# Block-causal attention and a gated feed-forward in fp32: the last part of the feed-forward in chunks of 512 tokens instead of 256

## The chip, the cores and the metric

The kernel runs on one core of one Trainium2 chip. The metric is the time of one execution in microseconds (us) of device time; lower is better. The core has five engines, each with a queue of its own that is worked through strictly in program order: PE (TensorE: matrix products; PEld is its loading of weights), DVE (VectorE), ACT (ScalarE), POOL (GpSimd) and SP (SyncE, which here issues nearly all transfers). Matrix products are written to PSUM, a memory of eight banks; one bank holds 512 fp32 numbers on each of 128 partitions. Everything else on the chip lies in SBUF, and the DRAM beside the chip holds inputs, outputs and scratch.

## The reference, cut to what matters

```python
# attention: q, k, v are [8, 8, 576, 64] (batch, heads, sequence, head size)
scores = scale * np.matmul(q, k.transpose(0, 1, 3, 2))
mask = pos[:, None] // 64 >= pos[None, :] // 64
scores = np.where(mask, scores, -1000000000.0)
attn = np.exp(scores - np.max(scores, axis=-1, keepdims=True))
attn = attn / (np.sum(attn, axis=-1, keepdims=True) + 1e-09)
x = np.matmul(attn, v)          # transposed and reshaped to [4608, 512]
# feed-forward: w_in is [512, 2048], w_out is [2048, 512]
h = x @ w_in
P = a[0] + a[1] * h + a[2] * h * h + a[3] * h * h * h
Q = 1.0 + np.abs(b[0]) * np.abs(h) + np.abs(b[1]) * h * h
out = (P / (Q + 1e-6)) @ w_out  # [4608, 512]
```

## The kernel before

Products are made in three parts of reduced fp32 each (high by high, high by low, low by high), so each operand is kept as a high and a low half, and every product below comes as three matmuls.

**Attention** goes over 32 pairs of heads. Its result x is written to scratch in DRAM (`xscr`, one tile for each batch, high and low halves side by side, transposed so that the 512 features lie on partitions in four blocks `dc`).

**The feed-forward** (class `Ffn`) is cut twice. Over the 2048 hidden features in two phases: phase 0 takes the first 10 blocks of 128 (`NFA`), phase 1 the last 6 (`NFB`). Over the 4608 tokens in 18 chunks of 256 (`CT`, `NCH`). A unit is one chunk and two blocks, so a chunk has 5 units in phase 0 and 3 in phase 1 (`NU`): 90 and 54 units. Phase 0 runs between the steps of the attention as its batches are finished, and its last units run when the attention has ended; phase 1 runs after the attention as a whole. Each unit has four steps, and `steps` writes them down with a lag of one, two and three units:

- `first`: 24 matmuls (L200), 2 blocks x 4 feature blocks x 3 parts, each 128x128 weights against 256 tokens, into one PSUM bank `h`; then ACT (L207, L208), POOL (L209, L210) and DVE (L211, L212) work out numerator and denominator. L212 is the last reader of `h`.
- `recip`: ACT (L217, L222) and DVE (L223 to L225) divide; in phase 1 the reciprocal `r` lies in a PSUM bank as well.
- `split`: ACT (L232) and POOL (L233) make the high and low half `gh` and `gl`.
- `second`: 12 matmuls (L249) of 512 columns add the unit's share to `o`, one bank for each 128 tokens, so two in a chunk, `o0` and `o1`. After a chunk's last unit phase 0 copies `o` to `os` (L256) and writes it to scratch `pscr`; phase 1 reads that partial sum back into `pt` (one buffer), adds it on DVE (L262) and writes the output.

Tokens are read from `xscr` by `load` (L184): a chunk has two tiles `x` of two feature blocks each, out of one ring of three buffers (`XB`) in the pool `ffn`.

**PSUM**: five banks in `ps_a` (scores, transposes and `pv` of the attention; later every second `h`, and all `r`), one in `ps_h` (the other `h`), two in `ps_o`.

**What sets the order.** The kernel is written in a Python order, and a scheduler then decides, from a timeline of its own, in which order each engine's instructions stand; buffers and waits follow from that, and on the chip nothing passes anything else on the same engine. All transfers named here stand in SP's queue. The completion marks of its transfers go round in eight lanes, and a transfer may be issued when the one eight places ahead of it has landed. When the attention ends, its SBUF pools are given back and the pools `wB` (weights of phase 1, twelve transfers of 512 KB, L586) and `ffb` (second set of buffers for the feed-forward) are laid in the same place; nothing can be written there before the attention's last readers are through.

Names below are `h0_15_4`: tile h, phase 0, chunk 15, unit 4; `x0_15_1` is the second tile of tokens of chunk 15; `o31_1` is the last product of the attention (`pv` of pair 31).

Of the kernel before, what the change touches and what calls it, by code (L numbers as in the profile page):

```python
# [9 lines left out]
F32 = mybir.dt.float32  # L10
F32R = mybir.dt.float32r
# [33 lines left out]
CBUFS = 2  # L45
NFA = 10
NFB = NF - NFA
NU = (NFA // 2, NFB // 2)
LP = 96
NL = S // LP  # L50
QSCALE = 0.125
# [7 lines left out]
def attn_ffn_kernel(  # L59
# [14 lines left out]
    cpool = ctx.enter_context(tc.tile_pool(name="const", bufs=1))  # L74
    dpool = ctx.enter_context(tc.tile_pool(name="scratch", bufs=1, space=DRAM))
    ffn = ctx.enter_context(tc.tile_pool(name="ffn", bufs=2))
    ps_a = ctx.enter_context(tc.tile_pool(name="ps_a", bufs=5, space=PSUM))
    ps_h = ctx.enter_context(tc.tile_pool(name="ps_h", bufs=1, space=PSUM))
    ps_o = ctx.enter_context(tc.tile_pool(name="ps_o", bufs=1, space=PSUM))

# [85 lines left out]
    class Ffn:  # L166
# [6 lines left out]
            self.ready = 0  # L173

        def load(self, ph, c):
            self.x[ph, c] = []
            for i in range(2):
                x = ffn.tile([128, 2, 2, CT], F32R, name=f"x{ph}_{c}_{i}", tag="x", bufs=XB)
                t0 = c * CT
                while t0 < (c + 1) * CT:  # L180
                    b = t0 // S
                    t1 = min((c + 1) * CT, (b + 1) * S)
                    for d in range(2):
                        nc.sync.dma_start(out=x[:, d, :, t0 - c * CT:t1 - c * CT].bitcast(F32),  # L184
                                          in_=xscr[b][:, 2 * i + d, :, t0 - b * S:t1 - b * S])
                    t0 = t1
                self.x[ph, c].append(x)

        def first(self, ph, c, u):
            wih, wil, _, _ = self.w[ph]  # L190
            xs = self.x[ph, c]
            tag = f"{ph}_{c}_{u}"
            pool = self.pools[self.n % len(self.pools)]
            h = self.hpools[self.n % len(self.hpools)].tile([128, 2, CT], F32, name=f"h{tag}", tag="a")
            for j in range(2):
                f = 2 * u + j
                fs = slice(f * 128, (f + 1) * 128)
                for dc in range(4):
                    for i, (w, hl) in enumerate(((wih, 1), (wih, 0), (wil, 0))):
                        nc.tensor.matmul(h[:, j, :], lhsT=w[:, dc, fs], rhs=xs[dc // 2][:, dc % 2, hl, :],  # L200
                                         start=(dc == 0 and i == 0), stop=(dc == 3 and i == 2))
# [10 lines left out]
            nc.vector.scalar_tensor_tensor(out=st, in0=st, scalar=a1, in1=hf, op0=ALU.subtract, op1=ALU.mult)  # L212
            self.m[ph, c, u] = (pool, ut, vt, st)

        def recip(self, ph, c, u):
            pool, ut, vt, st = self.m[ph, c, u]
            nc.scalar.activation(out=vt, in_=ut, func=AF.Ln, bias=qcb)  # L217
            if ph == 1:
                r0 = ps_a.tile([128, 512], F32, name=f"r{ph}_{c}_{u}", tag="a")
            else:  # L220
                r0 = vt
            nc.scalar.activation(out=r0, in_=vt, func=AF.Exp, scale=-1.0)  # L222
            nc.vector.scalar_tensor_tensor(out=ut, in0=ut, scalar=QC, in1=r0, op0=ALU.add, op1=ALU.mult)  # L223
            nc.vector.scalar_tensor_tensor(out=r0, in0=ut, scalar=-2.0, in1=r0, op0=ALU.add, op1=ALU.mult)  # L224
            nc.vector.scalar_tensor_tensor(out=st, in0=st, scalar=a0, in1=r0, op0=ALU.subtract, op1=ALU.mult)  # L225

        def split(self, ph, c, u):
            pool, ut, vt, st = self.m.pop((ph, c, u))
            tag = f"{ph}_{c}_{u}"
            gh = pool.tile([128, 2, CT], F32R, name=f"gh{tag}", tag="gh", bufs=GBUFS if pool is ffn else 2)  # L230
            gl = pool.tile([128, 2, CT], F32R, name=f"gl{tag}", tag="gl", bufs=GBUFS if pool is ffn else 2)
            nc.scalar.copy(out=gh.rearrange("p j t -> p (j t)"), in_=st)  # L232
            nc.gpsimd.tensor_tensor(out=gl.rearrange("p j t -> p (j t)"), in0=st,  # L233
                                    in1=gh.rearrange("p j t -> p (j t)").bitcast(F32), op=ALU.subtract)
            self.g[ph, c, u] = (gh, gl)

        def second(self, ph, c, u):
            _, _, woh, wol = self.w[ph]
            gh, gl = self.g.pop((ph, c, u))
            nu = NU[ph]  # L240
            if u == 0:
                self.o = [ps_o.tile([128, DM], F32, name=f"o{ph}_{c}_{m}", tag=f"o{m}")
                          for m in range(2)]
            for j in range(2):
                f = 2 * u + j
                for m in range(2):
                    ms = slice(m * 128, (m + 1) * 128)
                    for i, (g, w) in enumerate(((gl, woh), (gh, woh), (gh, wol))):
                        nc.tensor.matmul(self.o[m], lhsT=g[:, j, ms], rhs=w[:, f, :],  # L249
                                         start=(u == 0 and j == 0 and i == 0),  # L250
                                         stop=(u == nu - 1 and j == 1 and i == 2))
            if u == nu - 1:
                osb = ffn.tile([128, 2, DM], F32, name=f"os{ph}_{c}", tag="os")
                if ph == 0:
                    for m in range(2):
                        nc.scalar.copy(out=osb[:, m, :], in_=self.o[m])  # L256
                    nc.sync.dma_start(out=pscr[c], in_=osb)
                else:
                    part = ffb.tile([128, 2, DM], F32, name=f"pt{c}", tag="pt", bufs=1)
                    nc.sync.dma_start(out=part, in_=pscr[c])  # L260
                    for m in range(2):
                        nc.vector.tensor_tensor(out=osb[:, m, :], in0=self.o[m], in1=part[:, m, :], op=ALU.add)  # L262
                    nc.sync.dma_start(out=out[c * CT:(c + 1) * CT, :].rearrange("(m p) d -> p m d", p=128),
                                      in_=osb)
                self.o = None

        def steps(self):
            units = [(ph, c, u) for ph in range(2) for c in range(NCH) for u in range(NU[ph])]
            l1, l2, l3 = LAG
            for i in range(len(units) + l3):  # L270
                if i < len(units):
                    if units[i][:2] not in self.x:
                        self.load(*units[i][:2])
                    if i + 1 < len(units):
                        ph, c, u = units[i + 1]
                        if u == 0 and c < self.ready:
                            self.load(ph, c)
                if 0 <= i - l2 < len(units):
                    self.split(*units[i - l2])
                if i < len(units):  # L280
# [338 lines left out]
```

## Time and profile before

| | |
|---|---|
| median of 3 runs | 1389.79 us (1387.79 to 1392.57) |
| the profiled execution, its own time | 1388.67 us |
| its span, first to last instruction | 1386.9 us |
| mean granted TensorE clock | 0.971 |
| matmuls of L200 (`first`) | 3456, of 128x256 |
| matmuls of L249 (`second`) | 1728, of 128x512 |
| attention's last matmul | starts at 980.63 us of the span |

How to read it: a profile is one execution. The views used below are the page's busy time of each engine; tables of the busy time in stretches of the span; the chain of waits, which starts at the last instruction and goes back, at each step, to what released it; the waits in total; and the timeline, instruction by instruction. A matmul's own duration holds the time in which it flows through the array beside its neighbours; what it costs in a stream is the distance from its start to the next one's.

### The profile page before, as it was taken

Reading aid. Unit: us, or ns where it says so; the run is one execution under the profiler, and the core shown is the slowest. Engines: PE = TensorE matmul, PEld = TensorE weight load, DVE = VectorE, ACT = ScalarE, POOL = GpSimd, SP = SyncE. Lnnn points to the kernel's source line nnn. Section 1 sums busy time; section 2 is a strip of 40 time slices with the busy share of each in tenths; the row PEclk is TensorE's granted clock in tenths of the full one; section 3 lists DMA queues with packets and bytes.
Section 4 is the critical chain, followed back from the end, with each engine's and each line's share of the span. In section 5 each row is a group of like instructions: output and inputs, shape, how many; then the busy total and the mean of one; then the engine's idle time right before and its main releaser. Section 6 shows DMA issues by size and latency. Waiting matters only on the chain.

```text
span 1386.9 us, 25820 instructions
## 1 busy us (share of the span) xinstructions
PE 1296.0 (93%) x8736; PEld 1190.8 (86%) x8736; DVE 1031.0 (74%) x2048; ACT 909.3 (66%) x2250; POOL 958.3 (69%) x1240
## 2 busy tenths in 40 slices
PE   4778799999899989999999999999989999999998
PEld 3667788999888889888989999999979999999897
DVE  5898877787678868877767777766756677777665
ACT  5766766777577766776777777776545655555553
POOL 4888987687677757777767676766556655556564
PEclk9687999999999999999999999999999999999999
DMA  9778555666556665675654565651711333333332
GB/s 221 191 195 236 147 150 160 168 168 181 147 136 154 163 167 140 156 171 140 168 134 110 153 149 126 150 141 44 263 55 61 107 122 122 122 122 122 122 122 91
DMA packets 225635, 200.93 MB, mean 145 GB/s; under 512 B 132064, under 2 KB 195552, under 8 KB 225504
## 3 DMA queue, kind: packets, MB, share of 16 engines
q1 hardware_dynamic: 225440, 199.28, 53.8%
q8 instruction: 70, 1.15, 0.3%
q14 instruction: 61, 0.50, 0.1%
q0 software_dynamic: 64, 0.00, 0.0%
HBM read 98.57 MB, written 44.04 MB: 103 GB/s over the span
## 4 chain that ended last, share of the span: by engine, by line
PE 70%; DVE 9%; POOL 8%; ACT 5%; DMA 4%; issue 2%; SPq 1%; POOLq 0%; ACTq 0%; DVEq 0%
PE h L200 25%; PE o L249 25%; PE o L488 9%; PE t L469 4%; PE s L420 3%; PE s L421 3%; PE tp L354 2%; ACT p L437 1%; DVE v L224 1%; POOL u L210 1%; DVE nm L425 1%; POOL p L450 1%; DMA x<-xscr 1%; POOL gl L233 1%; DVE u L223 1%
## 5 line engine op out<-in xcount | busy, mean ns | idle before, releaser
L200 PE MATMUL h<-x,wih 128*128 128x256 f32 x2304 | 442.6, 288 | 10.1 <-DMA x<-xscr 5.9
L200 PEld LDWEIGHTS h<-x,wih 128*128 128x128 f32 x2304 | 368.8, 192 | 19.6 <-issue 6.8
L200 PE MATMUL h<-x,wil 128*128 128x256 f32 x1152 | 329.5, 286 | 0.0
L249 PE MATMUL o<-woh,gl 128*128 128x512 f32 x576 | 233.0, 405 | 8.1 <-POOL gl L233 6.8
L209 POOL TENSOR_SCALAR v<-u,bab 128x512 f32<-128x512 f32 x144 | 119.7, 831 | 162.9 <-ACT u L207 160.8
L249 PE MATMUL o<-woh,gh 128*128 128x512 f32 x576 | 228.5, 397 | 0.0
L249 PE MATMUL o<-wol,gh 128*128 128x512 f32 x576 | 227.2, 395 | 0.0
L233 POOL TENSOR_TENSOR gl<-s,gh 128x512 fp32r<-128x512 f32 x144 | 188.4, 1309 | 51.4 <-ACT gh L232 48.3
L425 DVE TENSOR_REDUCE nm<-s 128x1 f32<-128x288 f32 (+4 forms) x384 | 161.7, 427 | 81.2 <-PE s L424 46.1
L200 PEld LDWEIGHTS h<-x,wil 128*128 128x128 f32 x1152 | 221.3, 192 | 0.5
L437 ACT ACTIVATE p<-s,nm 128x288 f32<-128x288 f32 (+4 forms) x384 | 184.6, 485 | 48.4 <-DVE nm L425 34.9
L210 POOL TENSOR_TENSOR u<-v,u 128x512 f32<-128x512 f32 x144 | 189.7, 1318 | 9.8
L450 POOL TENSOR_SCALAR p<-p,rc 128x128 f32<-128x128 f32 (+3 forms) x256 | 166.2, 660 | 30.0 <-DVE rc L445 28.3
L217 ACT ACTIVATE v<-u,qcb 128x512 f32<-128x512 f32 x144 | 104.6, 726 | 95.9 <-POOL u L210 95.1
L207 ACT ACTIVATE u<-h 128x512 f32<-128x512 f32 x144 | 86.0, 597 | 120.8 <-PE h L200 114.4
L420 PE MATMUL s<-kq 128*128 128x256 f32 (+3 forms) x384 | 138.3, 362 | 22.0 <-DMA kq<-hl 9.6
L211 DVE TENSOR_TENSOR s<-s,h 128x512 f32<-128x512 f32 x144 | 98.6, 684 | 68.7 <-ACT s L208 67.9
L249 PEld LDWEIGHTS o<-woh,gl 128*128 128x128 f32 x576 | 109.5, 190 | 28.9 <-POOL gl L233 9.3
L249 PEld LDWEIGHTS o<-wol,gh 128*128 128x128 f32 x576 | 109.1, 189 | 22.8
L249 PEld LDWEIGHTS o<-woh,gh 128*128 128x128 f32 x576 | 109.5, 190 | 16.0
L421 PE MATMUL s<-kq 128*128 128x256 f32 (+3 forms) x384 | 121.0, 317 | 0.0
L469 PE MATMUL t<-ident,p 128*128 128x128 f32 (+1 forms) x672 | 114.0, 280 | 6.2 <-DVE x L492 1.8
(105 smaller groups left out, 3031.9 us busy)
## 6 DMA issues: line engine op xcount, KB each, us to landing
kq<-hl SPq DMA_DIRECT2D x64, 432.0 KB, 4.2
x<-xscr SPq DMA_DIRECT2D x96, 256.0 KB, 3.6
kq<-hl SPq DMA_DIRECT2D x64, 288.0 KB, 5.3
xscr<-x SPq DMA_DIRECT2D x32, 320.0 KB, 4.2
qr<-in_q_dram SPq DMA_DIRECT2D x64, 144.0 KB, 2.8
kr<-in_k_dram SPq DMA_DIRECT2D x64, 144.0 KB, 2.9
kq<-hl SPq DMA_DIRECT2D x64, 144.0 KB, 4.8
pscr<-os SPq DMA_DIRECT2D x18, 512.0 KB, 3.2
```

Of the source, the lines that this page charges most:

```text
L200: nc.tensor.matmul(h[:, j, :], lhsT=w[:, dc, fs], rhs=xs[dc // 2][:, dc % 2, hl, :], start=(dc == 0 and i == 0), stop=(dc == 3 and i == 2))
L209: nc.gpsimd.tensor_scalar(out=vt, in0=ut, scalar1=b1, scalar2=b0, op0=ALU.mult, op1=ALU.add)
L210: nc.gpsimd.tensor_tensor(out=ut, in0=vt, in1=ut, op=ALU.mult)
L233: nc.gpsimd.tensor_tensor(out=gl.rearrange("p j t -> p (j t)"), in0=st, in1=gh.rearrange("p j t -> p (j t)").bitcast(F32), op=ALU.subtract)
L249: nc.tensor.matmul(self.o[m], lhsT=g[:, j, ms], rhs=w[:, f, :], start=(u == 0 and j == 0 and i == 0), stop=(u == nu - 1 and j == 1 and i = ...
L420: nc.tensor.matmul(ps[:, :ww], lhsT=kq[:, 0, qs], rhs=kq[:, 1, c0:c0 + ww], start=True, stop=False)
L421: nc.tensor.matmul(ps[:, :ww], lhsT=kq[:, 0, qs], rhs=kq[:, 2, c0:c0 + ww], start=False, stop=not last)
L425: nc.vector.reduce_max(out=nm[:nq, j, i:i + 1], in_=ps[:nq, :w], axis=AX.X, negate=True)
L437: nc.scalar.activation(out=pt[:nq, j, c0:c0 + w], in_=banks[i][:nq, :w], func=AF.Exp, bias=nm[:nq, j, 0:1], scale=1.0, accum_out=sm[:nq, j ...
L450: nc.gpsimd.tensor_scalar(out=pt[:nq, jj, 64:n], in0=pt[:nq, jj, 64:n], scalar1=rc[:nq, jj:jj + 1], scalar2=1.0, op0=ALU.mult, op1=ALU.mult)
L469: nc.tensor.transpose(ps[:, i, :nq], src, ident[:nq, :nq])
L488: nc.tensor.matmul(o[:, s0:w], lhsT=vblock(vv, x), rhs=pp, start=(x == 0 and i == 0), stop=(x == nb - 1 and i == 2))
```

## The change

Phase 1 takes 9 chunks of 512 tokens and units of one block of hidden features, 6 to a chunk; the number of units stays 54. `first` makes 12 matmuls of 512 columns instead of 24 of 256. `second` still makes 12, now for one block and four groups of 128 tokens, into four banks `o0` to `o3`. The scalar work of a unit has the same 128x512 shape as before. A chunk's end now makes two outputs of 256 tokens each, one after the other, through the one buffer `pt`.

PSUM: `ps_a` is given back with the attention; a new pool `ps_b` takes its five banks: three for every second `h` and for all `r`, one each for `o2` and `o3`.

Tokens: a tile of phase 1 is one feature block of 512 tokens, four to a chunk. Tiles are taken by turns from `ffn` and from the last of the pools in use, with three buffers in each. Once the attention has ended that last pool is `ffb`, for phase 0 too: the second tile of each chunk that is loaded from then on lies in `ffb`.

```diff
+CTS, NBU = (CT, 512), (2, 1)
+NU = (NFA // NBU[0], NFB // NBU[1])
+NCS = (NT // CTS[0], NT // CTS[1])
...
-    ps_a = ctx.enter_context(tc.tile_pool(name="ps_a", bufs=5, space=PSUM))
...
         def load(self, ph, c):
+            n = CTS[ph]
+            nd = 512 // n
...
-                x = ffn.tile([128, 2, 2, CT], F32R, name=f"x{ph}_{c}_{i}", tag="x", bufs=XB)
+            for i in range(4 // nd):
+                pool = (ffn, self.pools[-1])[i % 2]
+                x = pool.tile([128, nd, 2, n], F32R, name=f"x{ph}_{c}_{i}", tag="x", bufs=XB)
...
         def first(self, ph, c, u):
-            h = self.hpools[self.n % len(self.hpools)].tile([128, 2, CT], F32, name=f"h{tag}", tag="a")
-            for j in range(2):
-                f = 2 * u + j
+            hp = self.hpools[self.n % len(self.hpools)]
+            h = hp.tile([128, NBU[ph], CTS[ph]], F32, name=f"h{tag}", tag="a", bufs=1 if hp is ps_h else 3)
+            for j in range(NBU[ph]):
+                f = NBU[ph] * u + j
...
-                r0 = ps_a.tile([128, 512], F32, name=f"r{ph}_{c}_{u}", tag="a")
+                r0 = ps_b.tile([128, 512], F32, name=f"r{ph}_{c}_{u}", tag="a", bufs=3)
...
         def second(self, ph, c, u):
+            nm = CTS[ph] // 128
             if u == 0:
-                self.o = [ps_o.tile([128, DM], F32, name=f"o{ph}_{c}_{m}", tag=f"o{m}")
-                          for m in range(2)]
+                self.o = [(ps_o if m < 2 else ps_b).tile([128, DM], F32, name=f"o{ph}_{c}_{m}", tag=f"o{m}", bufs=1)
+                          for m in range(nm)]
...
             if u == nu - 1:
+                for k in range(nm // 2):
+                    c2 = c * nm // 2 + k
...
-                    part = ffb.tile([128, 2, DM], F32, name=f"pt{c}", tag="pt", bufs=1)
-                    nc.sync.dma_start(out=part, in_=pscr[c])
+                        part = ffb.tile([128, 2, DM], F32, name=f"pt{c2}", tag="pt", bufs=1)
+                        nc.sync.dma_start(out=part, in_=pscr[c2])
...
-                        if u == 0 and c < self.ready:
+                        if u == 0 and c < self.ready and ph < len(self.pools):
...
     with ExitStack() as actx:
+        ps_a = actx.enter_context(tc.tile_pool(name="ps_a", bufs=5, space=PSUM))
...
-    ff.pools, ff.hpools = [ffn, ffb], [ps_h, ps_a]
+    ps_b = ctx.enter_context(tc.tile_pool(name="ps_b", bufs=1, space=PSUM))
+    ff.pools, ff.hpools = [ffn, ffb], [ps_h, ps_b]
```

What the scheduler makes of it. Up to the end of the attention every engine's order is the same as before. **SP, at the end of the attention.** These rows are SP's transfers, destination first, from the last but one product of the attention to the first transfers behind the weights of phase 1 (`wih10` to `wol10`, four for each pair of blocks). Before:

```order
L493 DMA xscr7_80<-x30_1_13239 128x2x256
L184 DMA x0_15_1_13752<-xscr6_79 128x2x192 x2
L184 DMA x0_15_1_13752<-xscr7_80 128x2x64
L184 DMA x0_16_0_14038<-xscr7_80 128x2x256 x2
L493 DMA xscr7_80<-x31_0_13430 128x2x320
L184 DMA x0_15_1_13752<-xscr7_80 128x2x64
L493 DMA xscr7_80<-x31_1_13548 128x2x256
L586 DMA wih10_13712<-wih10_198 128x4x256
...
L586 DMA wol10_13715<-wol10_201 128x1024
L260 DMA pt0_15031<-pscr0_81 128x1024
L257 DMA pscr14_95<-os0_14_13977 128x1024
L184 DMA x0_16_1_14041<-xscr7_80 128x2x256 x2
```

With the change:

```order
L504 DMA xscr7_77<-x30_1_13239 128x2x256
L189 DMA x0_16_0_14042<-xscr7_77 128x2x256 x2
L189 DMA x0_17_0_14329<-xscr7_77 128x2x256 x2
L504 DMA xscr7_77<-x31_0_13430 128x2x320
L504 DMA xscr7_77<-x31_1_13548 128x2x256
L598 DMA wih10_13713<-wih10_198 128x4x256
...
L598 DMA wol10_13716<-wol10_201 128x1024
L189 DMA x0_15_1_13756<-xscr6_76 128x2x192 x2
L189 DMA x0_15_1_13756<-xscr7_77 128x2x64 x2
L267 DMA pscr14_92<-os0_14_13981 128x1024
L189 DMA x0_16_1_14045<-xscr7_77 128x2x256 x2
```

The second tile of chunk 15 moved from ahead of the twelve weight transfers to right behind them, since it now lies in `ffb`.

**PE, at the same place.** The rows are matmuls, from the last one of the attention; each group of rows with the same `h` or `o` is cut to its first. Before:

```order
L488 MATMUL o31_1_13520<-pt2h_132,vpl_135 128x256
L200 MATMUL h0_15_0_13816<-x0_15_0_13747,wih0_142 128x256
...
L200 MATMUL h0_15_0_13816<-x0_15_1_13752,wih0_142 128x256 x2
...
L200 MATMUL h0_15_1_13871<-x0_15_1_13752,wih0_142 128x256 x2
...
L200 MATMUL h0_15_2_13926<-x0_15_0_13747,wih0_142 128x256 x2
...
L249 MATMUL o0_14_0_13733<-woh0_144,gl0_14_4_13868 128x512
...
L200 MATMUL h0_15_4_14048<-x0_15_0_13747,wih0_142 128x256 x2
...
L200 MATMUL h0_15_3_13985<-x0_15_0_13747,wih0_142 128x256 x2
```

With the change:

```order
L499 MATMUL o31_1_13520<-pt2h_132,vpl_135 128x256
L256 MATMUL o0_14_0_13737<-woh0_144,gl0_14_4_13872 128x512
...
L206 MATMUL h0_15_0_13820<-x0_15_0_13751,wih0_142 128x256 x2
...
L206 MATMUL h0_15_2_13930<-x0_15_0_13751,wih0_142 128x256 x2
...
L206 MATMUL h0_15_4_14052<-x0_15_0_13751,wih0_142 128x256 x2
...
L206 MATMUL h0_15_0_13820<-x0_15_1_13756,wih0_142 128x256 x2
L206 MATMUL h0_15_0_13820<-x0_15_1_13756,wil0_143 128x256
L206 MATMUL h0_15_1_13875<-x0_15_1_13756,wih0_142 128x256 x2
```

Between the attention's last matmul and the first that reads `x0_15_1` there now stand 12 matmuls of `second` (unit `14_4`) and six of `first` for each of the units 0, 2 and 4 of chunk 15; before, whole units stood there, one after the other.

**SP, at the very end.** The rows are the last transfers of the program. Before:

```order
L184 DMA x1_17_1_17721<-xscr7_80 128x2x256 x2
L263 DMA out_0_dram<-os1_15_17780 128x2x512
L260 DMA pt16_17957<-pscr16_97 128x1024
L263 DMA out_0_dram<-os1_16_17956 128x2x512
L260 DMA pt17_18015<-pscr17_98 128x1024
L263 DMA out_0_dram<-os1_17_18014 128x2x512
```

With the change:

```order
L189 DMA x1_8_3_16956<-xscr7_77 128x2x512
...
L273 DMA out_0_dram<-os1_15_17140 128x2x512
L270 DMA pt16_17333<-pscr16_94 128x1024
L273 DMA out_0_dram<-os1_16_17332 128x2x512
L270 DMA pt17_17339<-pscr17_95 128x1024
L273 DMA out_0_dram<-os1_17_17338 128x2x512
```

The sequence of names is the same, but `os1_16` and `os1_17` now belong to one chunk: both are added up behind the chunk's last unit, so `pt17` is read back after the end of the matmuls and no longer during them.

More of the change, by code (lines that the diff above doesn't have):

```diff
@@ L47 @@
 NFB = NF - NFA
-NU = (NFA // 2, NFB // 2)
+CTS, NBU = (CT, 512), (2, 1)
+NU = (NFA // NBU[0], NFB // NBU[1])
+NCS = (NT // CTS[0], NT // CTS[1])
 LP = 96
@@ L175, in load @@
         def load(self, ph, c):
+            n = CTS[ph]
+            nd = 512 // n
             self.x[ph, c] = []
-            for i in range(2):
-                x = ffn.tile([128, 2, 2, CT], F32R, name=f"x{ph}_{c}_{i}", tag="x", bufs=XB)
-                t0 = c * CT
-                while t0 < (c + 1) * CT:
+            for i in range(4 // nd):
+                pool = (ffn, self.pools[-1])[i % 2]
+                x = pool.tile([128, nd, 2, n], F32R, name=f"x{ph}_{c}_{i}", tag="x", bufs=XB)
+                t0 = c * n
+                while t0 < (c + 1) * n:
                     b = t0 // S
[L182 to L185, printed above, removed]
+                    t1 = min((c + 1) * n, (b + 1) * S)
+                    for d in range(nd):
+                        nc.sync.dma_start(out=x[:, d, :, t0 - c * n:t1 - c * n].bitcast(F32),
+                                          in_=xscr[b][:, nd * i + d, :, t0 - b * S:t1 - b * S])
                     t0 = t1
-                self.x[ph, c].append(x)
+                self.x[ph, c] += [x[:, d] for d in range(nd)]
         def first(self, ph, c, u):
@@ L199, in first @@
                     for i, (w, hl) in enumerate(((wih, 1), (wih, 0), (wil, 0))):
-                        nc.tensor.matmul(h[:, j, :], lhsT=w[:, dc, fs], rhs=xs[dc // 2][:, dc % 2, hl, :],
+                        nc.tensor.matmul(h[:, j, :], lhsT=w[:, dc, fs], rhs=xs[dc][:, hl, :],
                                          start=(dc == 0 and i == 0), stop=(dc == 3 and i == 2))
@@ L229, in split @@
             tag = f"{ph}_{c}_{u}"
-            gh = pool.tile([128, 2, CT], F32R, name=f"gh{tag}", tag="gh", bufs=GBUFS if pool is ffn else 2)
-            gl = pool.tile([128, 2, CT], F32R, name=f"gl{tag}", tag="gl", bufs=GBUFS if pool is ffn else 2)
+            gh = pool.tile([128, NBU[ph], CTS[ph]], F32R, name=f"gh{tag}", tag="gh", bufs=GBUFS if pool is ffn else 2)
+            gl = pool.tile([128, NBU[ph], CTS[ph]], F32R, name=f"gl{tag}", tag="gl", bufs=GBUFS if pool is ffn else 2)
             nc.scalar.copy(out=gh.rearrange("p j t -> p (j t)"), in_=st)
@@ L240, in second @@
             nu = NU[ph]
+            nm = CTS[ph] // 128
             if u == 0:
-                self.o = [ps_o.tile([128, DM], F32, name=f"o{ph}_{c}_{m}", tag=f"o{m}")
-                          for m in range(2)]
-            for j in range(2):
-                f = 2 * u + j
-                for m in range(2):
+                self.o = [(ps_o if m < 2 else ps_b).tile([128, DM], F32, name=f"o{ph}_{c}_{m}", tag=f"o{m}", bufs=1)
+                          for m in range(nm)]
+            for j in range(NBU[ph]):
+                f = NBU[ph] * u + j
+                for m in range(nm):
                     ms = slice(m * 128, (m + 1) * 128)
@@ L250, in second @@
                                          start=(u == 0 and j == 0 and i == 0),
-                                         stop=(u == nu - 1 and j == 1 and i == 2))
+                                         stop=(u == nu - 1 and j == NBU[ph] - 1 and i == 2))
             if u == nu - 1:
[L253 to L258, printed above, removed]
-                    part = ffb.tile([128, 2, DM], F32, name=f"pt{c}", tag="pt", bufs=1)
[L260 to L264, printed above, removed]
+                for k in range(nm // 2):
+                    c2 = c * nm // 2 + k
+                    o = self.o[2 * k:2 * k + 2]
+                    osb = ffn.tile([128, 2, DM], F32, name=f"os{ph}_{c2}", tag="os")
+                    if ph == 0:
+                        for m in range(2):
+                            nc.scalar.copy(out=osb[:, m, :], in_=o[m])
+                        nc.sync.dma_start(out=pscr[c2], in_=osb)
+                    else:
+                        part = ffb.tile([128, 2, DM], F32, name=f"pt{c2}", tag="pt", bufs=1)
+                        nc.sync.dma_start(out=part, in_=pscr[c2])
+                        for m in range(2):
+                            nc.vector.tensor_tensor(out=osb[:, m, :], in0=o[m], in1=part[:, m, :], op=ALU.add)
+                        nc.sync.dma_start(out=out[c2 * CT:(c2 + 1) * CT, :].rearrange("(m p) d -> p m d", p=128),
+                                          in_=osb)
                 self.o = None
         def steps(self):
-            units = [(ph, c, u) for ph in range(2) for c in range(NCH) for u in range(NU[ph])]
+            units = [(ph, c, u) for ph in range(2) for c in range(NCS[ph]) for u in range(NU[ph])]
             l1, l2, l3 = LAG
```

## The prediction

> **What bounds the kernel now.** First the busy times of the page, then the table of stretches, then the chain of waits; the change touches only what lies behind 980 us.
>
> ```profile
> PE 1296.0 (93%) x8736; PEld 1190.8 (86%) x8736; DVE 1031.0 (74%) x2048; ACT 909.3 (66%) x2250; POOL 958.3 (69%) x1240
> ```
>
> PE leads, but this is an average. In stretches (busy us and instructions of each engine, then granted clock, transfer share, GB/s):
>
> ```profile
> core 0: us, PE busy (x) PEld busy (x) DVE busy (x) ACT busy (x) POOL busy (x), PEclk, DMA share, GB/s
> 1000.00:1020.00 20.00, 17.96 (x97) 15.26 (x96) 7.33 (x10) 5.14 (x9) 8.46 (x8) 0.91 0.40 156
> 1020.00:1040.00 20.00, 16.27 (x103) 15.11 (x102) 15.41 (x20) 12.25 (x21) 14.66 (x11) 0.91 0.16 54
> 1200.00:1220.00 20.00, 20.00 (x127) 18.09 (x126) 14.51 (x22) 11.08 (x18) 11.40 (x11) 1.00 0.42 131
> ```
>
> Phase 1 (the last row is typical of 1060 to 1360) is bound by PE alone: it is never idle at full clock, and the next engine, DVE, has a quarter of its time free. Between 1000 and 1040 PE waits and loses clock. So the change has to be judged in three places: steady phase 1, the stretch behind the attention, and the end.
>
> **Steady phase 1: 24 narrow matmuls become 12 wide ones.** The chain runs on PE here:
>
> ```profile
> 1198.00 2.87 PE h L200 x24
> 1200.87 2.75 PE o L249 x12
> ```
>
> Twenty-four matmuls of 256 columns take 2.87 us, 0.120 each; twelve of 512 columns, each with its own weights, take 2.75, 0.229 each. The new `first` is twelve of 512 columns with their own weights, the form that L249 already has. I price it so: 2.87 - 2.75 = 0.12 us a unit, 54 units, **-6.5 us**. The pace of L249 itself has a spread (starts of the first and sixth of two groups):
>
> ```profile
> 1206.33 0.40 PE L249 MATMUL o<-woh,gl 128*128 128x512 f32 x1
> 1207.49 0.39 PE L249 MATMUL o<-wol,gh 128*128 128x512 f32 x1
> ...
> 1202.10 0.39 PE L249 MATMUL o<-woh,gl 128*128 128x512 f32 x1
> 1203.23 0.39 PE L249 MATMUL o<-wol,gh 128*128 128x512 f32 x1
> ```
>
> Five distances in 1.16 us are 0.232, in 1.13 us 0.226: the saving lies between 54 x (2.87 - 2.78) = 4.9 and 54 x (2.87 - 2.71) = 8.6 us.
>
> The Trainium skill has a rule against most of this: "TensorE: Matmul & The Clock Gate", section "Back-to-back issue gap", gives N / 2.4 + 2.5 ns at full clock. By it 24 x 109.2 and 12 x 215.8 ns are 2.62 and 2.59 us, and the change would save 0.03 us a unit, an estimate of 1.7 us in all. The rows above show 120 and 229 ns, so some 11 and 13 ns more for each matmul, and that is what halving their number saves; I keep the rows; by the rule the sum at the end would be 4.8 us higher.
>
> What could take this back is a new wait. The guard on early loads and the three banks that `h` and `r` now share (five before) I cost at nothing: with ACT at 11 and DVE at 15 of 20 us both are read out long before PE comes round again; were it not so, each 0.1 us a unit would cost 5. Tokens:
>
> ```profile
> PE h L200 <- DMA x<-xscr: 0.7, 1, 0.7
> L184 SPq DMA_DIRECT2D x<-xscr x81: 359/467/1419, 1099.9 to 1353.4; - x81
> ...
> DMA to landing us min/median/max: 1.9/3.2/4.7
> ```
>
> Only one load was late, by 0.7 us. With the change the third tile of the next chunk takes the buffer that the last unit's first three matmuls release, and 34 or so wide matmuls (7.8 us) lie between that and its first reader; a load needs 4.7 at most. So **-0.7 us**, and no new wait.
>
> The banks `o2` and `o3`: the second read of `pt` can be issued only when both adds of the first half are done.
>
> ```profile
> L262 DVE TENSOR_TENSOR os<-o,pt 128x512 f32<-128x512 f32 x32 | 22.0, 688 | 1.3
> 1374.68 0.38 SPq L263 DMA_DIRECT2D out_dram<-os  x1
> 1375.16 0.41 SPq L260 DMA_DIRECT2D pt<-pscr  x1
> ...
> L260 SPq DMA_DIRECT2D pt<-pscr x17: 335/467/1376, 1103.7 to 1375.2; - x17
> ...
> DMA to landing us min/median/max: 3.8/4.4/5.5
> ```
>
> From the last matmul of `o1`: about 0.2 until DVE starts, 0.69 for its add, 0.5 until SP has sent the output and issues `pt`, 4.4 to landing: 5.8 us; with two adds more, 7.2. In the order PE has 42 or 48 matmuls of 0.229 us before the next chunk asks for `o2`, 9.6 or 11.0 us. The cover is 2.4 us at the tighter ones (four of eight): I cost it at nothing. While DVE waits for `pt`, L212 of the next unit but one stands behind the add, and with it the release of an `h` that PE wants three steps later; DVE's free quarter pays for that. If the cover went, a microsecond too late costs a microsecond at each of four places, 4 us at most by the 5.5 us landing and a delayed DVE.
>
> **Behind the attention: a tile of tokens behind twelve weight transfers.** The change also moves the second tile of chunk 15 (`x0_15_1`) from ahead of the weights in SP's queue to behind them. SP before, and the landing of the last weight transfer:
>
> ```profile
> 984.00 0.60 SPq L586 DMA_DIRECT2D wih<-wih  x1
> ...
> 995.28 0.43 SPq L586 DMA_DIRECT2D wol<-wol  x1
> ...
> DMA to landing us min/median/max: 9.1/9.1/9.1
> ...
> 1000.00:1007.00 7.00, 7.00 (x38) 5.92 (x37) 5.50 (x8) 2.63 (x5) 4.40 (x4) 1.00 1.04 404
> ```
>
> The transfers are saturated there (share 1.04, 404 GB/s), and the last weights land at 995.28 + 9.1 = 1004.4. `x0_15_1` is issued behind them; the three of its four pieces that the first reader needs are 0.46 MB, 1.1 us at 404 GB/s: 1005.5. PE gets there much sooner:
>
> ```profile
> 980.63 0.28 PE L488 MATMUL o<-pt2h,vpl 128*128 128x256 f32 x1
> ...
> 978.56 1.29 POOL L233 TENSOR_TENSOR gl<-s,gh 128x512 fp32r<-128x512 f32 x1 [4.08 <-ACT gh L232]
> ```
>
> The attention's last matmul ends at 980.75; four narrow ones that stood ahead of it have moved behind, so 980.3, and the whole scene, the weights too, is 0.5 earlier: the tile is there at 1005.0. In between PE has 12 wide matmuls (their `gl` is ready at 979.9) and 18 narrow ones, 2.75 + 2.16 = 4.9 us, up to 985.2. Everything behind in PE's queue waits with it, and DVE, ACT and POOL, fed by it, run dry. Idle: **19.8 us**. Where the nearest rows put the ends: the four token loads issued from 997.1 to 1002.1 took 7.4 to 10.4 us, and a load on a free system 3.2:
>
> ```profile
> L184 SPq DMA_DIRECT2D x<-xscr x4: 359/366/371, 997.1 to 1002.1; - x4
> ...
> DMA to landing us min/median/max: 7.4/9.5/10.4
> ```
>
> Issued up to about 997.5, that is 1000.7 to 1007.9, an idle time of 15.5 to 22.7. And PE restarts at half clock. What the kernel loses there today:
>
> ```profile
> 1009.50 0.65 PE L249 MATMUL o<-woh,gl 128*128 128x512 f32 x1 [2.04 <-POOL gl L233]
> ...
> PE h L200 <- DVE s L212: 3.7, 1, 3.7
> ...
> 1010.00:1012.00 2.00, 2.00 (x6) 1.59 (x5) 0.00 (x0) 0.00 (x0) 0.67 (x1) 0.50 0.00 0
> 1009.50 4.60 PE o L249 x12
> 1032.10 4.07 PE h L200 x23
> 1036.17 3.19 PE o L249 x12
> ...
> 1367.73 2.89 PE h L200 x24
> ...
> 1377.93 1.29 POOL L233 TENSOR_TENSOR gl<-s,gh 128x512 fp32r<-128x512 f32 x1 [3.18 <-ACT gh L232]
> ...
> 993.74 1.67 DVE L224 SCALAR_TENSOR_TENSOR v<-u,v 128x512 f32<-128x512 f32 x1
> ```
>
> Waits of 2.0 and 3.7 us, each with a restart at clock 0.50: 4.60 instead of 2.75 us, then 4.07 and 3.19 instead of 2.75 twice; 1.85 + 1.32 + 0.44 = 3.6. Together 9.4 us. I take these as gone: after the long wait PE has four `first` to finish (72 matmuls) and then `16_1`, `15_3` and `16_3` before it needs a `gl` of chunk 15, 144 x 0.120 = 17 us, and the chain of one unit from the end of `h` to `gl` through ACT, POOL and DVE takes 8.6 (the kernel's last unit: 1370.6 to 1379.2). But four units come to those engines nearly at once, and DVE's operations stretch when it is crowded (L224 1.67 us, against 0.69 for an add of the same shape above), so I leave 1 us for a wait, between 0 and the 5.8 of today. One restart costs 1.8. Sum: 19.8 + 1.8 + 1 - 9.4 = **+13.2 us**.
>
> **The end.** The last matmuls, the two adds, the output:
>
> ```profile
> 1379.28 2.38 PE o L249 x9
> 1381.68 1.38 DVE os L262 x2
> 1383.09 0.38 SPq L263 DMA_DIRECT2D out_dram<-os  x1
> ```
>
> Before, `pt17` was loaded at 1375.16, under the matmuls, and the adds end 0.9 us after the last matmul (1382.2). With the change `pt17` waits for the first half's adds, which end 0.5 before the last matmul (`o1` is done 6 x 0.229 before it). Then 0.5 for SP, 4.4 to landing, 1.4 for two adds: 5.8 us after the last matmul instead of 0.9, **+4.9 us** (4.3 to 6.0 by the landing). Nothing hides it.
>
> **Sum**, against the profiled execution's own 1388.67 us (1.1 below the median of the runs, 1389.79): -6.5 - 0.7 + 13.2 + 4.9 = +10.9, **1399.6 us**. The work saved in phase 1 is smaller than what one tile's new place in a queue costs.
>
> **The rivals.** *The tile is not late* (8%): it lands as soon as in a free system, PE idles 15.5 us: 1395.3; were it there before 985, the stretch would cost nothing, or even save today's 9.4. For it: transfers are cut over 16 engines and might pass each other. Against it: the loads issued at 997 to 1002 took 9.5 us, not 3.2. *The crowd behind the wait* (10%): the four units arrive together, DVE and POOL stretch, PE waits as long as today, 5.8 instead of 1, and gaps of 1 us open at the chunk ends: 1404 to 1408. For it: the row of 1020 to 1040 has DVE at 15.4 and POOL at 14.7 of 20. Against it: 17 us of PE work lie ready. *The other side, faster*: a wide matmul of `first` is paced by its weight load and not by its columns. A load takes
>
> ```profile
> L200 PEld LDWEIGHTS h<-x,wih 128*128 128x128 f32 x2304 | 368.8, 192 | 19.6 <-issue 6.8
> ```
>
> 0.192 us; then 12 take 2.30, 54 units save 30.8 and the time is 1375. It decides from below 0.206 us a matmul, where the saving passes 21.5 us. Against it: L249 has loads as long and stands at 0.229. The page cited above also names 131 ns for sustained N=512; no row here comes near it. 4%.
>
> **How the numbers follow.** A measurement of this kernel can tell about 0.3% from no change: 1385.6 to 1394.0. Forecast 78%, between 1393 and 1405 by the spreads of its terms; a tenth of it, with the saving at its high end and little waiting, lies inside 0.3%. Of the early tile's 8% some 6 lie there; the crowd's 10% are slower, the last rival's 4% faster. Faster 4%, within 14%, slower 82%. Eight in ten: from 1391, which takes in an early tile with the best saving, to 1408.
>
> **What would show it.** Right: wide matmuls of `first` 0.226 to 0.232 us apart; PE idle for some 20 us from about 985, released by a transfer of `x`, with DVE, ACT and POOL idle beside it; no wait of 3.7 us at 1028; in the last 10 us a transfer of `pt` between two pairs of adds. Wrong: PE busy through 985 to 1005; waits of PE for DVE's adds at the chunk ends; a time below 1391, which would mean that the tile came early or that narrow matmuls had cost more than I read.

## The result and the profile after

The changed kernel takes 1400.78 us (median of 8 runs, 1397.71 to 1402.17), the kernel before 1390.01 us beside it (1387.79 to 1396.95). The ratio is 1.0064 (95% interval 1.0044 to 1.0085): slower, by more than the 0.3% that can be told from no change. The prediction was 1399.6 us, and slower with a chance of 82%.

Clock and busy times in stretches of the changed kernel; columns as in the prediction's table. The first two rows are the stall and the restart behind it, the last one is steady phase 1.

```profile
core 0: us, PE busy (x) PEld busy (x) DVE busy (x) ACT busy (x) POOL busy (x), PEclk, DMA share, GB/s
985.00:1007.00 22.00, 2.61 (x21) 2.33 (x19) 0.00 (x0) 1.00 (x2) 0.00 (x0) 0.63 0.94 342
1007.00:1011.00 4.00, 3.97 (x18) 4.00 (x19) 0.00 (x0) 0.00 (x0) 0.00 (x0) 0.50 0.99 364
...
1020.00:1040.00 20.00, 20.00 (x137) 18.53 (x136) 18.55 (x21) 13.82 (x23) 18.16 (x13) 1.00 0.17 54
...
1200.00:1220.00 20.00, 20.00 (x90) 16.57 (x89) 15.30 (x24) 11.36 (x19) 12.87 (x12) 1.00 0.59 192
```

In the row from 985 to 1007 us PE works off what it still has, up to 987.6, and ACT two instructions; then all four compute engines stand still, while the transfers run at 342 GB/s. Then come 4 us at clock 0.50, and a stretch in which PE is never idle and DVE and POOL are nearly full. In steady phase 1 PE is busy throughout, as before, but with 90 matmuls in 20 us instead of 127. PE's waits behind the attention, in total:

```profile
PE h L206 <- DMA pscr<-os: 19.4, 1, 19.4
PE o L256 <- POOL gl L239: 4.0, 4, 2.2
```

The timeline shows the long one on PE and what SP issued meanwhile, and the view of the source line gives the landings of the four pieces of `x0_15_1`:

```profile
987.33 0.28 PE L206 MATMUL h<-x,wil 128*128 128x256 f32 x1
1007.03 0.77 PE L206 MATMUL h<-x,wih 128*128 128x256 f32 x2 [19.42 <-DMA pscr<-os]
...
997.28 2.93 SPq L189 DMA_DIRECT2D x<-xscr  x4
1001.26 0.43 SPq L267 DMA_DIRECT2D pscr<-os  x1
...
L189 SPq DMA_DIRECT2D x<-xscr x4: 359/424/569, 997.3 to 999.9; - x4
...
DMA to landing us min/median/max: 7.0/8.3/8.6
```

The releaser is given as `pscr<-os`, but the matmul that waits reads `x`, and that tile is issued from 997.3 to 999.9 and lands 7.0 to 8.6 us later, the last piece at about 1006.9. The transfer that is named, issued at 1001.26, takes 6.8 us to land, so it lands at 1008.1, after PE has gone on, and can't have released it. In e2 below the same wait of PE stands under its own name:

```profile
pscr<-os SPq DMA_DIRECT2D x1, 512.0 KB, 6.8
...
PE h L206 <- DMA x<-xscr: 19.8, 1, 19.8
```

A releaser is inferred by the profile; the operand of the waiting instruction, and the landings, tell which transfer it was.

The chain in steady phase 1, and at the end:

```profile
1299.41 5.44 PE h L206 x24
1304.85 5.44 PE o L256 x24
...
1388.32 0.69 DVE os L272
...
1389.02 0.70 DVE os L272
...
1389.74 0.38 SPq L273
...
1390.17 3.98 DMA pt<-pscr
...
1394.23 0.69 DVE os L272
```

Wide matmuls stand 0.2267 us apart in `first` and in `second` alike. At the end the transfer of the last partial sum lies on the chain, 4.0 us between two pairs of adds, where the kernel before had matmuls.

### The profile page after: what moved, and what is told of

The parts are those of the page before. It is cut to its first block, busy times and chain, and to the rows that moved or that the text cites. A ratio compares the mean times of both kernels' runs of the same rounds, so it can differ in the third digit from the quotient of the medians.

```text
span 1399.4 us, 24412 instructions
## 1 busy us (share of the span) xinstructions
PE 1283.4 (92%) x8088; PEld 1156.5 (83%) x8088; DVE 1023.7 (73%) x2048; ACT 910.5 (65%) x2250; POOL 960.2 (69%) x1240
## 4 chain that ended last, share of the span: by engine, by line
PE 67%; POOL 10%; DVE 9%; DMA 6%; ACT 4%; issue 3%; SPq 2%; POOLq 0%; DVEq 0%; ACTq 0%
PE h L206 23%; PE o L256 22%; PE o L499 9%; PE t L480 4%; PE s L431 3%; PE s L432 3%; POOL gl L239 2%; PE tp L365 2%; DMA kq<-hl 2%; POOL u L216 1%; POOL v L215 1%; POOL p L461 1%; DVE u L229 1%; DVE v L230 1%; DMA xscr<-x 1%
## 5 line engine op out<-in xcount | busy, mean ns | idle before, releaser
L206 PE MATMUL h<-x,wih 128*128 128x256 f32 (+1 forms) x1872 | 418.2, 314 | 27.1 <-DMA pscr<-os 19.4
L206 PEld LDWEIGHTS h<-x,wih 128*128 128x128 f32 x1872 | 311.9, 192 | 47.3 <-issue 25.1
L206 PE MATMUL h<-x,wil 128*128 128x256 f32 (+1 forms) x936 | 291.7, 312 | 0.0
L215 POOL TENSOR_SCALAR v<-u,bab 128x512 f32<-128x512 f32 x144 | 122.6, 851 | 104.3 <-ACT u L213 99.0
L206 PEld LDWEIGHTS h<-x,wil 128*128 128x128 f32 x936 | 179.9, 192 | 8.8
L238 ACT CAST gh<-s 128x512 fp32r<-128x512 f32 x144 | 89.2, 623 | 72.6 <-DVE s L231 68.6
```

Source lines behind the costliest of these rows:

```text
L206: nc.tensor.matmul(h[:, j, :], lhsT=w[:, dc, fs], rhs=xs[dc][:, hl, :], start=(dc == 0 and i == 0), stop=(dc == 3 and i == 2))
```

## The experiments

Seven kernels separate the terms of the sum, an eighth asks what stretches the units behind the stall. Ratios are to the kernel before on the same chip.

**e1_tile_ffn: the tile back in `ffn`.**

```diff
-                pool = (ffn, self.pools[-1])[i % 2]
+                pool = (ffn, self.pools[-1])[i % 2] if ph == 1 else ffn
```

> The changed kernel, but the second token tile of phase 0's chunks stays in the pool ffn, as before the change; everything of phase 1 stays changed. Theory (the stall behind the attention is one tile's place in SP's queue): the 19.4 us in which PE is idle from 987 us go, with the 2.0 us of its restart and the 4.0 us of waits behind it, and the waits and restarts of the kernel before come back there, 9.4 us: 1400.8 - 25.4 + 9.4 = 1384.8 us; up to 2.6 us more if the second tile of chunk 16, which now stands behind four tiles of phase 1 (1 MB at 404 GB/s), comes late. Rival A (the stall comes from memory being laid out anew for 512-token chunks, PSUM and ffb, whichever tile is named): a stall of over 10 us stays, 1397 to 1401 us.

Measured: 1381.79 us, ratio 0.9933 (0.9909 to 0.9957). PE's waits from 975 us on:

```profile
PE o L256 <- POOL gl L239: 6.5, 3, 4.7
PE h L206 <- DVE s L218: 0.9, 1, 0.9
```

No wait for a transfer is left, so the second tile of chunk 16 was not late either. Waits for `gl` and DVE like those of the kernel before are back; the time is 3.0 us lower than worked out. In the profiled executions 2.4 us lie in the attention, whose last matmul starts at 980.1 us here and at 982.4 in the changed kernel. One line turns a kernel that is 0.6% slower than before into one that is 0.7% faster: rival A falls.

**e6_tile_first: the tile in `ffb`, but loaded ahead of the weights.** (The second hunk only keeps `steps` from loading the chunk a second time.)

```diff
+    ff.load(0, 15)
     for f in range(0, NFB, 2):
...
-                        if u == 0 and c < self.ready and ph < len(self.pools):
+                        if u == 0 and c < self.ready and ph < len(self.pools) and (ph, c) not in self.x:
```

> The changed kernel, with the tile x0_15_1 still in ffb, but its load written ahead of the twelve weight transfers. Theory (place in the queue): the tile is issued some 2.3 us behind the attention's last matmul, when its space comes free, at 984 to 986 us, and lands 4 to 5 us later, so PE, which runs dry 4.9 us behind that matmul, waits 2 to 6 us instead of 19.4: 1384 to 1389 us, the upper end if waits for gl like those of the kernel before (2.0 and 3.7 us) come back. Rival A (the space in ffb is what it waits for, not the queue): the tile lands no sooner, PE idles over 10 us, 1396 to 1401 us.

Measured: 1385.62 us, 0.9968 (0.995 to 0.9986). Waits, and the landing of the tile's four pieces:

```profile
PE h L206 <- DVE s L218: 5.6, 1, 5.6
PE h L206 <- DMA x<-xscr: 2.0, 1, 2.0
...
L189 SPq DMA_DIRECT2D x<-xscr x4: 360/462/467, 983.5 to 984.9; - x4
...
DMA to landing us min/median/max: 2.4/2.6/2.7
```

The same tile in the same space, issued in front, lands within 2.7 us, sooner than the 4 to 5 expected, and PE waits 2.0 us for it instead of 19.4. So the space in `ffb` costs about 2 us and the place in the queue the rest. A wait of 5.6 us for DVE comes later: PE loses 13.4 us up to 1080 here and 10.6 in e1 (counted as in the point-by-point section), which is most of the 3.8 us by which e1 is faster.

**e4_before_tile: the kernel before with that one move.**

```diff
-                x = ffn.tile([128, 2, 2, CT], F32R, name=f"x{ph}_{c}_{i}", tag="x", bufs=XB)
+                pool = (ffn, self.pools[-1])[i % 2] if ph == 0 else ffn
+                x = pool.tile([128, 2, 2, CT], F32R, name=f"x{ph}_{c}_{i}", tag="x", bufs=XB)
```

> The kernel before, with one thing of the change: the second token tile of phase 0's chunks is taken from ffb once the attention has ended. Chunks of 256 tokens, units of two blocks and PSUM are as before. Theory: PE idles some 19 to 20 us from about 985 us, with a restart of 2 us and some 4 us of waits behind it, in place of the 9.4 us lost today: 1390.0 + 16 = 1406 us, 1402 to 1409. Rival A (the stall needs the 512-token layout): 1390 us, within 2.

Measured: 1410.18 us, 1.0138 (1.0104 to 1.0172). The longest of PE's waits:

```profile
PE h L201 <- DMA pscr<-os: 18.4, 1, 18.4
```

With chunks of 256 tokens and PSUM as before, the stall is there all the same. The time is 1 us above the range that was expected: PE loses 7.9 us from 1015 to 1080 us behind the stall, the changed kernel 4.2 (counted as in the point-by-point section).

**e5_narrow: the changed kernel with 24 narrow matmuls in `first`.**

```diff
-                for dc in range(4):
-                    for i, (w, hl) in enumerate(((wih, 1), (wih, 0), (wil, 0))):
-                        nc.tensor.matmul(h[:, j, :], lhsT=w[:, dc, fs], rhs=xs[dc][:, hl, :],
-                                         start=(dc == 0 and i == 0), stop=(dc == 3 and i == 2))
+                for k in range(CTS[ph] // CT):
+                    ks = slice(k * CT, k * CT + CT)
+                    for dc in range(4):
+                        for i, (w, hl) in enumerate(((wih, 1), (wih, 0), (wil, 0))):
+                            nc.tensor.matmul(h[:, j, ks], lhsT=w[:, dc, fs], rhs=xs[dc][:, hl, ks],
+                                             start=(dc == 0 and i == 0), stop=(dc == 3 and i == 2))
```

> The changed kernel, but first() of phase 1 makes 24 matmuls of 256 columns again, two halves of 256 tokens one after the other, with the same tiles, banks, transfers and units. Theory (what phase 1 saves is the number of matmuls): 54 units take 24 x 0.120 instead of 12 x 0.2267, 0.15 us, and the switches from narrow to wide take 0.03 us a unit again: +0.18 x 54 = +9.6 us, 1410 us; a matmul of second() starts slower by 6 to 9 ns behind the narrow ones. Rival B (a matmul costs its columns and 2.5 ns, the saving comes from the loads and units laid out anew): +1.7 us, 1402.5 us, with 24 narrow ones at no more than 2.75 us.

Measured: 1409.79 us, 1.0137 (1.0109 to 1.0165), above the changed kernel by 9.0 us by the medians and by 10.1 by the ratios. The chain in its steady phase 1:

```profile
1299.30 2.87 PE h L208 x24
1302.17 0.69 PE o L258 x3
...
1305.74 1.39 PE o L258 x6
```

Twenty-four narrow matmuls again take 2.87 us, and `second` is dearer too: six wide matmuls directly behind narrow ones take 1.39 us, 0.232 each, where the changed kernel has 0.2267 throughout. So the saving comes with the number of matmuls, and a part of it lies in `second`, which was not touched: rival B falls. Each of these matmuls also brings a weight load of its own, and no run separates the two. By the formula that the Trainium skill, "TensorE: Matmul & The Clock Gate", section "Back-to-back issue gap", gives for the gap of isolated matmuls, this experiment would have cost an estimate of 1.7 us; the measurement decides against it here.

**e2_sum_in_os: the partial sum read straight into `os`.**

```diff
-                        part = ffb.tile([128, 2, DM], F32, name=f"pt{c2}", tag="pt", bufs=1)
-                        nc.sync.dma_start(out=part, in_=pscr[c2])
+                        nc.sync.dma_start(out=osb, in_=pscr[c2])
                         for m in range(2):
-                            nc.vector.tensor_tensor(out=osb[:, m, :], in0=o[m], in1=part[:, m, :], op=ALU.add)
+                            nc.vector.tensor_tensor(out=osb[:, m, :], in0=o[m], in1=osb[:, m, :], op=ALU.add)
```

> The changed kernel, but the partial sum is read from scratch straight into the output tile os (two buffers) and added to in place, so both halves of a chunk can be read before the chunk ends; pt is gone. Theory (the end waits for the second partial sum, 4.5 us longer than before the change): in the last 10 us no transfer of a partial sum stands between the two pairs of adds, the last add ends 1.4 to 1.6 us behind the last matmul instead of 5.6, and 1400.8 becomes 1396.8 us (1396 to 1398); the stall behind the attention stays at 19 to 20 us. Rival C (the write of the last output sets the end, the partial sum is hidden in it): 1400.8, within 1 us.

Measured: 1394.27 us, 1.0035 (1.002 to 1.005), below the 1396 to 1398 that were expected. Against the changed kernel the medians differ by 6.5 us, the ratios by 0.29% or 4.0 us. The end in the timeline:

```profile
1385.87 2.73 DVE L271 TENSOR_TENSOR os<-o,os 128x512 f32<-128x512 f32 x4 [3.68 <-PE o L256]
...
1387.27 1.75 SPq L272 DMA_DIRECT2D out_dram<-os  x2
1387.48 0.39 PE L256 MATMUL o<-wol,gh 128*128 128x512 f32 x1
```

Four adds in a row end at 1388.6, 1.1 us behind the start of the last matmul. The span ends at 1392.5, 5.0 us behind that start; in the changed kernel it is 9.4. Rival C falls. How much of the 6.5 us belongs to the edit beyond these 4.4 stays open; the attention alone ended 2.9 us earlier in this profile, with the same instructions.

**e3_tile_and_os: e1 and e2 together.**

> Both at once: the second tile of phase 0 stays in ffn (1381.8 us alone) and the partial sum is read into os. Theory: the two terms lie at different places and add up: 1381.8 - 4.0 = 1377.8 us, 13 us below the kernel before (ratio 0.9905). Rival C: 1381.8.

Measured: 1377.71 us, 0.9909 (0.9892 to 0.9925). The terms add up, and this kernel is faster than both: 12 us below the kernel before by the medians, 23 below the changed one.

**e7_tile_after_four: the tile behind four of the twelve transfers.** (With the same change of `steps` as in e6.)

```diff
     for f in range(0, NFB, 2):
+        if f == 2:
+            ff.load(0, 15)
```

> The changed kernel with the load of x0_15_1 written behind the first four of the twelve weight transfers. Theory (the tile waits for the bytes ahead of it): four transfers are 2.1 MB, 5.2 us at 404 GB/s, on top of the 2.0 us that PE waits with none ahead: PE idles 7.2 us (6.5 to 8) from about 985 us, on the line between none ahead (2.0 us) and twelve (19.4 us), which gives 7.8. Rival D (only the time that SP takes to issue what stands ahead counts, 2.5 us for four): 4.5 us. The time of the kernel: 1385.6 + 5.2 = 1390.8 us, less by up to 4 if the waits behind the stall shrink as they do in the changed kernel.

Measured: 1387.12 us, 0.9977 (0.9961 to 0.9993). PE's first wait, the tile's landing, and the stretches while it waits:

```profile
995.32 0.77 PE L206 MATMUL h<-x,wih 128*128 128x256 f32 x2 [9.13 <-DMA wih<-wih]
...
L189 SPq DMA_DIRECT2D x<-xscr x4: 378/468/470, 987.0 to 988.5; - x4
...
DMA to landing us min/median/max: 6.6/7.0/7.1
...
986.00:988.00 2.00, 0.19 (x2) 0.00 (x0) 0.00 (x0) 0.00 (x0) 0.00 (x0) 1.00 0.95 280
988.00:990.00 2.00, 0.00 (x0) 0.00 (x0) 0.00 (x0) 0.00 (x0) 0.00 (x0) 1.00 1.06 366
990.00:992.00 2.00, 0.00 (x0) 0.00 (x0) 0.00 (x0) 0.00 (x0) 0.00 (x0) 0.75 0.94 349
992.00:994.00 2.00, 0.00 (x0) 0.00 (x0) 0.00 (x0) 0.00 (x0) 0.00 (x0) 0.50 1.08 337
994.00:996.00 2.00, 0.68 (x3) 0.71 (x4) 0.00 (x0) 0.00 (x0) 0.00 (x0) 0.50 1.10 381
```

The wait grows with what stands ahead, 2.0, 9.1 and 19.4 us for none, four and twelve transfers, but 9.1 is more than the 6.5 to 8 expected, and rival D's 4.5 is further off. The expectation had divided by 404 GB/s and given the whole rate to the tile and what stands ahead. These rows, up to the tile's landing at 995.1, add up to 3.1 MB at some 340 GB/s, and the tile and the four transfers ahead of it are 2.6 MB. By an estimate from these figures the lower rate costs about 1 us (2.1 MB in 6.2 us and not 5.2), and the other 0.5 MB, nearly all of it of the transfers issued next, about 1.4; together that is near the 1.9 us by which 9.1 passes 7.2. No run separates the two. The time is lower than 1390.8 since the waits behind the stall are shorter, as in the changed kernel.

**e8_r_in_psum: e3, and phase 0's reciprocal behind the attention in a PSUM bank.**

```diff
-            if ph == 1:
+            if len(self.hpools) > 1:
                 r0 = ps_b.tile([128, 512], F32, name=f"r{ph}_{c}_{u}", tag="a", bufs=3)
```

> The kernel with both edits (1377.7 us), and in addition the reciprocal of phase 0's units behind the attention lies in a PSUM bank, as phase 1's does already. The waits of PE behind the attention there are 7.2 us, nearly all for gl. Theory (the waits come from DVE and POOL stretching while both operands of L229 to L231 lie in SBUF: 870 to 1090 ns on DVE against 682 to 745 with r in PSUM, L216 and L239 on POOL 1409 and 1548 against 1296): from 985 to 1060 us these groups fall to 680 to 750 ns and about 1300, a unit's chain gets some 1.2 us shorter and the crowd drains faster: the waits shrink by 2 to 6 us, 1372 to 1376 us. Rival E (the waits come from the order in which PE takes the units, all of first() late and at once, whatever an operation takes): the groups may shrink, the waits stay within 1 us, 1377 to 1378.

Measured: 1376.58 us, 0.9906 (0.988 to 0.9931), not to be told from e3 and between the two ranges that were expected. Two groups of instructions from 985 to 1060 us, first in e3, whose reciprocal is `v` in SBUF (busy us, mean ns of one), with its waits for `gl`:

```profile
L239 POOL TENSOR_TENSOR gl<-s,gh 128x512 fp32r<-128x512 f32 x12 | 18.5, 1548 | 14.9 <-ACT gh L238 14.9
L231 DVE SCALAR_TENSOR_TENSOR s<-s,coef,v 128x512 f32<-128x512 f32 x12 | 13.1, 1089 | 0.2
...
PE o L256 <- POOL gl L239: 6.3, 4, 4.0
```

and in e8, where it is `r` in PSUM, with PE's longest waits:

```profile
L239 POOL TENSOR_TENSOR gl<-s,gh 128x512 fp32r<-128x512 f32 x15 | 19.3, 1296 | 17.0 <-ACT gh L238 17.0
L231 DVE SCALAR_TENSOR_TENSOR s<-s,coef,r 128x512 f32<-128x512 f32 x13 | 9.6, 744 | 0.2
...
PE h L206 <- DVE s L218: 3.0, 1, 3.0
PE o L256 <- POOL gl L239: 1.3, 1, 1.3
```

Both engines' operations fall to the length that they have in phase 1 of e3 (745 and 1296 ns), and the waits for `gl` go from 6.3 to 1.3 us, as the theory had it. But the scheduler also moved 33 matmuls (6.5 us) from ahead of the attention's last one to behind it, a wait of 3.0 us for DVE, up to 983.6 us, has come, and the sum of all waits falls only from 7.2 to 5.5. That the stretching goes with where the reciprocal lies is shown; what it costs in time isn't, since the order changed with it, and the two kernels' times can't be told apart. The Trainium skill, "SBUF — State Buffer", section "SBUF: two separate sides", says that a DVE instruction with two inputs in SBUF and a GpSimd instruction that reads SBUF lock each other out of a shared port; the trace agrees in that both get longer, 1089 against 744 ns and 1548 against 1296.

## Why the prediction was right, point by point

The two profiled executions are 12.5 us apart in time and in span (1386.9 and 1399.4). For the split below every matmul behind the attention's last one is counted at 0.120 us (256 columns) or 0.227 (512), and what the timeline has beyond that is lost time. The rows that bound the pieces, before and after, each the last matmul of the attention or of the program:

```profile
1381.94 0.39 PE L249 MATMUL o<-wol,gh 128*128 128x512 f32 x1
```

```profile
982.44 0.28 PE L499 MATMUL o<-pt2h,vpl 128*128 128x256 f32 x1
...
1389.95 0.39 PE L256 MATMUL o<-wol,gh 128*128 128x512 f32 x1
```

| piece | on record | measured |
|---|---|---|
| attention's last matmul (980.63 to 982.44) | 0 | +1.8 |
| lost by PE from there to 1080 (9.9 to 25.8) | +13.2 | +15.9 |
| the rest up to the last matmul: steady phase 1, late load, last wait | -7.2 | -9.7 |
| last matmul to the end of the span (5.0 to 9.4) | +4.9 | +4.5 |
| sum | +10.9 | +12.5 |

- **Attention's end.** Hardly the change: the orders are the same up to there but for a few matmuls, and e1, e2 and e4 to e7, where this holds too, start that matmul between 979.6 and 981.0. I take it as the spread of one execution. The other three pieces make +10.7 us, and the medians differ by 10.8.
- **The stall.** Right in place, cause and size: up to 1007.03, 19.4 us for 19.8, both ends some 2 us later than forecast, as the attention's end is, with 1.9 us lost in the restart for 1.8. e1, e6 and e4 show that one tile's place in SP's queue makes it. Behind the whole backlog the arithmetic with bytes and rate held; e7 shows that it comes out short for a part of the backlog.
- **The wait left behind the stall.** Mis-sized. I left 1 us; a wait of 2.2 us at 1044 and a restart at half clock behind it lose 4.1:

```profile
1044.13 0.50 PE L256 MATMUL o<-woh,gl 128*128 128x512 f32 x1 [2.20 <-POOL gl L239]
...
1045.40 0.63 PE L256 MATMUL o<-wol,gh 128*128 128x512 f32 x1
1045.82 0.63 PE L256 MATMUL o<-woh,gl 128*128 128x512 f32 x1
```

  The crowd that I gave 10% as a rival is there (DVE and POOL over 18 of 20 us busy from 1020 to 1040). It costs 3.1 us more than forecast, where the rival had 4.4 to 8.4; no gaps of 1 us opened at the chunk ends.
- **Steady phase 1.** Mis-sized, in the other direction. The step that failed: I gave the new wide matmuls the pace that L249 had, 2.75 us for twelve. That pace held the cost of following narrow ones. With only wide ones a unit takes 2 x 2.72 instead of 2.87 + 2.75 us, so 0.18 us less and not 0.12: 54 times that is 9.7, not 6.5. e5 shows it by putting the narrow ones back. The two figures that the prediction took for a spread of L249, 0.232 and 0.226, are this difference: the first is from matmuls right behind narrow ones, the second from the later half of a group. The rival of the weight load falls, since the wide ones stand at 0.2267 and not at 0.192; and its saving would have had to pass 20.5 us (1399.6 + 6.5 - 1385.6), not 21.5, to be told from no change.
- **The late load of tokens** is gone, as said. The forecast had no new wait for `gl` here; in front of the last twelve matmuls there is one:

```profile
1387.32 0.50 PE L256 MATMUL o<-woh,gl 128*128 128x512 f32 x1 [0.87 <-POOL gl L239]
```

- **Banks and guards at no cost.** Right: DVE does wait for the second partial sum at some chunk ends (below, from 1150 to 1250 us), but PE waits nowhere for it.

```profile
DVE os L272 <- DMA pt<-pscr: 1.5, 3, 0.7
```

- **The end.** Right: 4.5 for 4.9, and e2 takes it away. The forecast had its last adds 5.8 us behind the last matmul; the second pair starts at 1394.2 and ends at 1395.5, 5.6 us behind that matmul's start.

The two mis-sized terms, some 3 us each and in opposite directions, nearly cancel, so the closeness of 1399.6 to 1400.8 is partly luck. The forecast's direction isn't: it rests on the stall and on the end, which outweigh the saving in any of these sizes.

## What to carry to other kernels

A tile's pool can decide more than its address. Here the pool lay in space that came free late, the tile's load moved in the queue behind the weights that were written earlier for the same space, and a 0.5 MB tile behind 6 MB of weights waited for nearly all of them. When a buffer moves, read the queue's order around it, and put the load whose reader comes first in front. And price a new instruction in the surroundings that it will have: the pace of the same form in today's mix can hold the cost of its neighbours.

## What the runs showed of the hardware

- Matmuls of 512 columns, each with its own weights, stand 0.2267 us apart among themselves and 0.232 on average for the first six behind matmuls of 256 columns, which stand 0.120 apart.
- After a wait of only 2.2 us PE started at full pace and fell to half clock 1.3 us later (1044.13 to 1045.40 above, then 0.42 us between starts; the granted clock is 0.50 from 1046 to 1048).
- The same four pieces of a tile land 2.4 to 2.7 us after issue with no weights ahead (e6), 6.6 to 7.1 behind four weight transfers (e7), 7.0 to 8.6 behind twelve. Of the 19.4 us that PE waits in the changed kernel, half passes while SP issues the twelve, up to 997.3, and half with the tile under way.
